# A retention layer with its FFN: the first 512 tokens as two units of 256, two tokens to a partition, and the FFN begun on the first unit

## The chip, the cores and the metric

The kernel runs on one core of one Trainium2 chip. The time is the device time of an execution in microseconds (us). Before the change the median of three runs is 356.64 us (356.58 to 357.01). Beside the times there is one profiled execution, from which every duration below is read.

## What is computed

Eight batches of 576 tokens with eight heads of 64 channels go through retention (attention without a softmax, the scores weighted by a power of the distance), and the result through a bilinear FFN:

```python
scores = scale * np.matmul(q, k.transpose(0, 1, 3, 2))      # B, H, S, D = 8, 8, 576, 64
gamma = 1.0 - 2.0 ** (-5.0 - np.arange(H))
rel = pos[:, None] - pos[None, :]
Dmat = np.where(rel >= 0, gamma[:, None, None] ** rel[None], 0.0)
attn = np.matmul(scores * Dmat[None], v)
x = attn.transpose(0, 2, 1, 3).reshape(B * S, H * D)        # 4608 x 512
out = ((x @ w_a) * (x @ w_b)) @ w_out                       # 512 -> 1536 -> 512
```

Inputs and output are float32; the products run in bfloat16.

## The kernel before

**Retention by chunks.** The 4608 tokens are 36 chunks of 128 tokens, a chunk two half steps of 64; nine half steps are a batch. The decay is factored: row j of v is multiplied by gamma to the power -j (table `vs`), row i of the result by gamma to the power i (table `qs`), so that only a 0/1 mask (`keep`) stands between. For a chunk, `load_qk` brings q and k with a cast to bf16 (GpSimd's queue), `load_v` brings v in float32 (SyncE's queue), `vscale` makes `vb` from `vf` and `vs`, `transposes` turns q and k over (by TensorE and two copies in the first chunks, by a DMA transpose on SyncE's queue from chunk 6), and `kv` forms k'v for each half step. The sums of these over a batch are the state: each sum (`s`, on VectorE, in a pool of three buffers) is cast to bf16 (`sbf`). `stage1` takes the products of q with the state and the scores `sc`, which VectorE masks into `sT`; `stage2` adds the products of `sT` with `vb` and the rest of the state products, and VectorE multiplies with `qs` into `xT`, the FFN's input, transposed. `kv` leaves its sums in a list `later`; `pop` takes one off at set places in the FFN, `flush` takes all.

**FFN by blocks.** Nine blocks of 512 tokens. `ffn_ab` runs twelve groups: four products with `wa_sb` into `pa`, cast by ScalarE into `ha`; four with `wb_sb` into `pb`; VectorE multiplies the two into `hT`. `ffn_out` takes four rows of 128 tokens with twelve products each into `po`, copied to `osb` by ScalarE and VectorE in turn and stored by SyncE. All of `pa`, `pb`, `po` and the transposes `tp` share four PSUM buffers (tag `ab`).

**What sets the order.** Each engine does its instructions in the order in which the program writes them. The front (chunks 0 to 3) is written out: four chunks one after the other, with `idle_products` (products of zeros) before and after, `hold` (a tiny DMA that makes SyncE's queue wait for a load), and the weights in four pieces of `load_w`. Then a table `todo` of (cost, function, unit) is worked off while the FFN runs: `run` adds up the cost of each product (1.0 for 512 columns) and calls the functions whose cost is reached at the next edge. Chunks 4 and 5 are units of their own, from 6 on a unit is two chunks:

```python
todo = [(52, begin_single, (4,)), (58, first, (4,)), (68, second, (4,)),
        (56, make_qs, (EARLY, QCOLS)),
        (80, begin_single, (5,)), (86, first, (5,)), (94, second, (5,)),
        (130, first, (6,)), (150, second, (6,))]
```

`begin_single` is vscale, transposes and kv of a chunk; `first` is stage1 and, through `ahead`, the transposes of the next unit, vscale of the one after on GpSimd, and loads of the fourth after; `second` is stage2 and kv of the next unit. A block has 144 such cost units: 96 of `ffn_ab`, 48 of `ffn_out`.

## Time and profile before

| What | us |
|---|---|
| median of three runs | 356.64 |
| profiled execution, in all | 358.02 |
| its span, first to last instruction | 356.3 |
| first FFN product | 28.28 |
| block 2 begins | 114.89 |
| last `ffn_out` begins | 342.20 |

The span is what the views divide up. TensorE (PE) is busy for 329.1 us of it, VectorE (DVE) 167.6, ScalarE (ACT) 93.5, GpSimd (POOL) 133.4. A busy TensorE is not one at its peak: the same product can take twice as long, which shows in the distance between starts and not in the share. In rows of the timeline the first two numbers are start and length in us, the brackets give the idle time before and what ended it; in rows of groups the numbers behind the bar are busy us, mean ns of one, and idle time before with its releasers.

### The profile page before, as it was taken

Reading aid. Unit: us, or ns where it says so; the run is one execution under the profiler, and the core shown is the slowest. Engines: PE = TensorE matmul, PEld = TensorE weight load, DVE = VectorE, ACT = ScalarE, POOL = GpSimd, SP = SyncE. Lnnn points to the kernel's source line nnn. Section 1 sums busy time; section 2 is a strip of 40 time slices with the busy share of each in tenths; the row PEclk is TensorE's granted clock in tenths of the full one; section 3 lists DMA queues with packets and bytes.
Section 4 is the critical chain, followed back from the end, with each engine's and each line's share of the span. In section 5 each row is a group of like instructions: output and inputs, shape, how many; then the busy total and the mean of one; then the engine's idle time right before and its main releaser. Section 6 shows DMA issues by size and latency. Waiting matters only on the chain.

```text
span 356.3 us, 8899 instructions
## 1 busy us (share of the span) xinstructions
PE 329.1 (92%) x3739; PEld 168.3 (47%) x3739; DVE 167.6 (47%) x321; ACT 93.5 (26%) x179; POOL 133.4 (37%) x196
## 2 busy tenths in 40 slices
PE   5559877599999999999999999999999999999995
PEld 2433434584774444444444445444444444444442
DVE  4652445343573456445553554464436534533321
ACT  3621363231220331132113211321232022212321
POOL 8765528932544604920554066307400310100000
PEclk9999999889999999999999999999999999999999
DMA  9999999999999990996199929966930140011002
GB/s 112 181 195 184 180 186 154 161 162 148 134 155 218 159 138 8 177 165 127 43 170 157 111 36 196 156 89 86 177 65 2 61 119 2 2 67 53 2 29 89
DMA packets 155624, 41.48 MB, mean 116 GB/s; under 512 B 145216, under 2 KB 151104, under 8 KB 155584
## 3 DMA queue, kind: packets, MB, share of 16 engines
q0 software_dynamic: 80944, 14.16, 51.2%
q1 hardware_dynamic: 74496, 26.62, 38.5%
q8 instruction: 29, 0.48, 0.5%
q10 hardware_dynamic: 144, 0.13, 0.1%
q14 instruction: 11, 0.09, 0.1%
HBM read 37.75 MB, written 9.44 MB: 132 GB/s over the span
## 4 chain that ended last, share of the span: by engine, by line
PE 84%; DMA 4%; DVE 4%; POOL 3%; issue 3%; ACT 1%; POOLq 0%; SPq 0%; DVEq 0%
PE pa L365 26%; PE pb L373 26%; PE po L390 25%; DMA vf<-in_v_dram 3%; POOL qk L102 2%; PE o L332 2%; PE o L290 2%; PE kv L257 2%; DVE s L270 1%; DMA qk<-in_q_dram 1%; PE sc L310 1%; DVE hT L378 1%; ACT qs L193 1%; DVE vb L219 1%; POOL vb L219 1%
## 5 line engine op out<-in xcount | busy, mean ns | idle before, releaser
L378 DVE TENSOR_TENSOR hT<-ha,pb 128x512 bf16<-128x512 bf16 (+2 forms) x126 | 76.9, 611 | 107.5 <-PE pb L373 100.5
L365 PE MATMUL pa<-xT,wa_sb 128*128 128x512 bf16 (+2 forms) x504 | 117.6, 358 | 4.7 <-DVE hT L378 3.9
L373 PE MATMUL pb<-xT,wb_sb 128*128 128x512 bf16 (+2 forms) x504 | 116.5, 355 | 0.0
L370 ACT CAST ha<-pa 128x512 bf16<-128x512 f32 (+2 forms) x126 | 66.0, 525 | 159.7 <-PE pa L365 159.6
L390 PE MATMUL po<-wo_sb,hT 128*128 128x512 bf16 x432 | 97.3, 379 | 0.0
L277 POOL CAST sbf<-s 128x256 bf16<-128x256 f32 x53 | 21.0, 403 | 154.7 <-DVE s L270 103.8
L373 PEld LDWEIGHTS <-wb_sb 128*128 128x128 bf16 x504 | 49.4, 101 | 47.4 <-issue 1.9
L365 PEld LDWEIGHTS <-wa_sb 128*128 128x128 bf16 x504 | 47.6, 101 | 48.8 <-issue 6.5
L390 PEld LDWEIGHTS <-hT 128*128 128x128 bf16 x432 | 41.1, 98 | 47.6
L102 POOL DMA_DIRECT2D qk<-in_q_dram x40 | 35.0, 877 | 8.5 <-issue 4.0
L102 POOL DMA_DIRECT2D qk<-in_k_dram x40 | 34.2, 859 | 8.0 <-DMA qk<-in_q_dram 4.9
L406 ACT COPY osb<-po 128x512 f32<-128x512 f32 x18 | 10.6, 586 | 80.1 <-PE po L390 80.1
L408 DVE COPY osb<-po 128x512 f32<-128x512 f32 x17 | 11.8, 692 | 41.5 <-PE po L390 41.5
L219 POOL TENSOR_TENSOR vb<-vf,vs 128x512 bf16<-128x512 f32 x30 | 30.6, 1039 | 0.0
L349 DVE TENSOR_TENSOR xT<-o,qs 128x512 bf16<-128x512 f32 (+1 forms) x42 | 23.8, 608 | 8.7 <-PE o L290 4.5
L318 DVE TENSOR_TENSOR sT<-sc,keep 128x512 bf16<-128x512 f32 (+1 forms) x42 | 23.8, 609 | 7.7 <-PE sc L310 7.6
L270 DVE TENSOR_TENSOR s<-kv,s 128x256 f32<-128x256 f32 x56 | 23.6, 421 | 7.0 <-POOL sbf L277 4.0
L290 PE MATMUL o<-qkT,sbf 64*64 64x64 bf16 x512 | 16.2, 201 | 7.3 <-DVE xT L349 5.0
L290 PEld LDWEIGHTS <-sbf 64*64 64x64 bf16 x512 | 10.9, 111 | 14.2 <-ACT sbf L275 5.6
L257 PE MATMUL kv<-vb,qk 64*64 64x64 bf16 x512 | 9.9, 203 | 6.5 <-DVE vb L219 5.4
L332 PEld LDWEIGHTS <-vb 64*64 64x64 bf16 x576 | 7.8, 113 | 10.4 <-issue 10.4
L332 PE MATMUL o<-sT,vb 64*64 64x64 bf16 x576 | 10.1, 200 | 2.5 <-DVE sT L318 2.4
(44 smaller groups left out, 92.5 us busy)
## 6 DMA issues: line engine op xcount, KB each, us to landing
out_dram<-osb SPq DMA_DIRECT2D x35, 256.0 KB, 2.8
vf<-in_v_dram SPq DMA_DIRECT2D x32, 256.0 KB, 6.1
qk<-in_q_dram POOLq DMA_DIRECT2D x32, 128.0 KB, 6.2
qk<-in_k_dram POOLq DMA_DIRECT2D x32, 128.0 KB, 7.0
wo_sb<-in_moe_w_out_dram POOLq DMA_DIRECT2D x3, 512.0 KB, 16.1
vf<-in_v_dram SPq DMA_DIRECT2D x8, 128.0 KB, 5.4
wa_sb<-in_moe_w_a_dram POOLq DMA_DIRECT2D x4, 192.0 KB, 8.0
wb_sb<-in_moe_w_b_dram POOLq DMA_DIRECT2D x4, 192.0 KB, 8.2
```

The costliest lines, as they stand in the source:

```text
L102: nc.gpsimd.dma_start(t[r0:r0 + n, w, :].rearrange("p (h d) -> p h d", h=H), src[b, :, s0:s0 + n, :].rearrange("h s d -> s h d"))
L219: eng.tensor_tensor(vb.rearrange("p (h d) -> p h d", h=H), vf.rearrange("p (h d) -> p h d", h=H), vs[:, i % PER, :].unsqueeze(2).to_broadc ...
L270: nc.vector.tensor_tensor(new, ps[s][:, ci], last_sum[0], op=ALU.add)
L290: nc.tensor.matmul(o[s][half(c), ci, j, :], st[half(r), p, :], qkt_of[i][half(r), 0, p, half(s)], start=start, stop=True, skip_group_check ...
L318: nc.vector.tensor_tensor(sT[:, r].rearrange("p n c t -> p (n c) t"), sc[r].rearrange("p n c t -> p (n c) t"), keep.unsqueeze(1).to_broadc ...
L332: nc.tensor.matmul(o[s][half(c), ci, j, :], vb[half(s), 64 * h:64 * h + 64], sT[half(s), h % 2, ci, h // 2, :], start=False, stop=True, sk ...
L349: nc.vector.tensor_tensor(view(xT, t0), o[s].rearrange("p n j t -> p j n t"), view(qs, c0), op=ALU.mult)
L365: nc.tensor.matmul(pa[:, 0:n], wa_sb[:, c, fs], xT[:, c, tok0:tok0 + n], start=(c == 0), stop=(c == NC - 1))
L370: nc.scalar.copy(ha[:, 0:n], pa[:, 0:n])
L373: nc.tensor.matmul(pb[:, 0:n], wb_sb[:, c, fs], xT[:, c, tok0:tok0 + n], start=(c == 0), stop=(c == NC - 1))
L378: nc.vector.tensor_tensor(hT[:, F, off:off + n], ha[:, 0:n], pb[:, 0:n], op=ALU.mult)
L390: nc.tensor.matmul(po, hT[:, F, u * 128:(u + 1) * 128], wo_sb[:, F, :], start=(F == 0), stop=(F == NF - 1))
```

## The change

The first 512 tokens (all of batch 0, bar its last 64) are no longer four chunks but two units u of 256 tokens, with two neighbouring tokens on a partition, so that a row of a load is 128 floats instead of 64. Everything for them has functions of its own (`fresh_...`). Their states are summed in PSUM (`kv_sum`) and cast by ScalarE from there. v of all chunks is loaded on GpSimd's queue instead of SyncE's, and `vf`, `vb` get more buffers. The FFN's groups 0 to 2 (`NF1 = 3`) run on unit 0, then on unit 1, in 256 columns; from group 3 on block 0 runs in 512. Chunks 4 and 5 move from `ffn_ab` of block 0 into its `ffn_out`, block 1's first half runs as twelve groups of 256 in place of twelve of 128 and six of 256, and each `first` and `second` gets a new place. `transposed` and `scale_v` are the DMA transposes and GpSimd's vscale of a unit; in `todo` a unit's number from 6 on is that of a pair, number 6 being chunks 6 and 7, number 7 chunks 8 and 9. kv now runs two units ahead, its casts one step after their sums. Identity, masks and ramps are made by VectorE's compares and by GpSimd ramps in float32.

```diff
-    vf_pool = pool("vf", 5)
-    vb_pool = pool("vb", 6)
+    vf_pool = pool("vf", 6)
+    vb_pool = pool("vb", 8)
...
     def load_v(i):
...
-            nc.sync.dma_start(
+            nc.gpsimd.dma_start(
...
+    load_fresh_v(0, 0, 4, nc.sync)
+    load_fresh_qk(0)
+    ramp(idx[:, 0:512], [[1, 512]], 0, 0)
+    ramp(posf[:, 0:4], [[1, 2], [256, 2]], 0, 2)
+    ramp(posf[:, 4:4 + MID + 1], [[128, MID + 1]], 0, 1)
+    load_fresh_v(0, 4, 8, nc.gpsimd)
+    ramp(posf[:, 4 + MID + 1:NPOS], [[128, PER - MID - 1]], 64, 1)
+    load_fresh_qk(1)
+    load_fresh_v(1, 0, 8, nc.gpsimd)
+    load_w(0, 128)
+    load_w(128, 384)
+    load_w(384, 768)
...
+    nc.vector.tensor_scalar(identity, idx[:, 0:128], rowf[:, 2:3], None,
+                            op0=ALU.is_equal)
...
-    idle_products(7)
-    for i in range(4):
-        vscale(i, nc.vector)
-        transposes(i, False)
-        kv((i,), nc.scalar)
-        flush()
...
+    NF1 = 3
+    idle_products(36)
+    fresh_vscale(0, 0, 4)
+    fresh_transposes(0, idle_products)
+    idle_products(8)
+    make_qs(256, 512)
+    fresh_scores(0)
+    fresh_kv(0, 0)
+    idle_products(4)
+    fresh_state1(0)
+    fresh_kv(0, 1)
+    ramp(idx[:, 512:S], [[1, S - 512]], 512, 0)
+    load_w(768, 1152)
+    load_w(1152, DFF)
+    idle_products(8)
+    fresh_transposes(1, None)
+    idle_products(4)
+    fresh_vscale(1, 0, 8)
+    settled(0)
+    fresh_stage2(0)
+    idle_products(4)
+    fresh_scores(1)
+    fresh_kv(1, 0)
+    run_all(ffn_ab(0, 0, 256, 0, 1))
+    fresh_state1(1)
+    fresh_kv(1, 1)
+    state_of[8] = fresh_state[4]
+    run_all(ffn_ab(0, 0, 256, 1, NF1))
+    settled(1)
+    fresh_stage2(1)
+    run_all(ffn_ab(0, 256, 256, 0, NF1))
...
+    load_wo(0, NF)
...
     def first(g):
         flush()
         stage1(units[g])
-        ahead(g)
+        if g >= 6:
+            if g + 2 < len(units):
+                transposed(g + 2)
+                scale_v(g + 2)
+            if g + 3 < len(units):
+                load(*units[g + 3])
...
     def second(g):
...
-        if 6 <= g + 1 < len(units):
-            kv(units[g + 1], nc.gpsimd)
+        if 8 < g + 2 < len(units):
+            kv(units[g + 2], nc.gpsimd)
...
+    load(*range(4, 10))
+    todo = [(60, make_qs, (512, S)), (64, make_qs, (S, 2 * S)),
+            (68, make_qs, (2 * S, QCOLS)),
+            (104, begin_single, (4,)), (110, first, (4,)), (118, second, (4,)),
+            (124, begin_single, (5,)), (130, first, (5,)),
+            (138, second, (5,)),
+            (139, scale_v, (6,)), (139, transposed, (6,)),
+            (140, load, (10, 11)), (145, scale_v, (7,)),
+            (148, kv, (units[6], nc.scalar)), (150, transposed, (7,)),
+            (166, first, (6,)), (180, second, (6,)),
+            (188, kv, (units[7], nc.scalar)),
+            (208, kv, (units[8], nc.scalar))]
...
-            todo += [(p - 86, first, (g,)), (p - 66, second, (g,))]
+            todo += [(p - 64, first, (g,)), (p - 50, second, (g,))]
...
-            todo += [(p - 40, first, (g,)), (p - 20, second, (g,))]
+            todo += [(p - 34, first, (g,)), (p - 18, second, (g,))]
...
-    at = [0.0]
-    run(ffn_ab(0, 0, 512, 0, NF))
-    run(ffn_ab(1, 512, 128, 0, 6))
-    run(ffn_ab(1, 640, 128, 0, 6))
-    run(ffn_ab(1, 512, 256, 6, NF))
+    at = [8.0 * NF1]
+    run(ffn_ab(0, 0, 512, NF1, NF))
     run(ffn_out(0))
+    run(ffn_ab(1, 512, 256, 0, NF))
     run(ffn_ab(1, 768, 256, 0, NF))
```

Three places in the order show what moves. The first is VectorE's queue up to the FFN's first `hT`. Before, the last of four chunks stands there (`vb`, its transposed k, two sums, the `xT` of the chunk ahead, two masks of its own, its `xT`):

```order
L219 TENSOR_TENSOR vb<-vf,vs 128x512
L241 COPY qkT<-tp 128x512
L270 TENSOR_TENSOR s_493<-kv_475,s_400 128x256
L270 TENSOR_TENSOR s_497<-kv_476,s_493 128x256
L349 TENSOR_TENSOR xT<-o_430,qs 128x4x64
L349 TENSOR_TENSOR xT<-o_431,qs 128x4x64
L318 TENSOR_TENSOR sT<-sc_537,keep 128x256
L318 TENSOR_TENSOR sT<-sc_538,keep 128x256
L349 TENSOR_TENSOR xT<-o_527,qs 128x4x64
L349 TENSOR_TENSOR xT<-o_528,qs 128x4x64
```

In the changed kernel the same queue holds unit 0's masks (`fsT`), unit 1's v (`fvb`), unit 0's `xT`, unit 1's masks, then the first three `hT`:

```order
L493 COPY fT<-ftp 128x1024
L546 TENSOR_TENSOR fsT<-fsc_280,keep_165 128x512
L546 TENSOR_TENSOR fsT<-fsc_281,keep_165 128x512
L546 TENSOR_TENSOR fsT<-fsc_301,keep_165 128x512
L546 TENSOR_TENSOR fsT<-fsc_302,keep_165 128x512
L462 TENSOR_TENSOR fvb<-vf_106,vs_all 128x512 x2
L568 TENSOR_TENSOR xT<-fo_344,qs 128x4x128
L568 TENSOR_TENSOR xT<-fo_345,qs 128x4x128
L546 TENSOR_TENSOR fsT<-fsc_482,keep_165 128x512
L546 TENSOR_TENSOR fsT<-fsc_483,keep_165 128x512
```

The sums have left VectorE, its instructions are twice as wide, and the masks of unit 1 stand between the first `xT` and the first `hT`.

The second place is GpSimd's queue around the first products on v. Before, from the scaled v of chunks 6 to 9 on (`qk` are loads of chunks 12 and 13, `vb` the scaled v, `sbf` casts of the state):

```order
L219 TENSOR_TENSOR vb<-vf,vs 128x512 x4
L102 DMA qk<-in_q_dram 128x8x64
L102 DMA qk<-in_k_dram 128x8x64
L102 DMA qk<-in_q_dram 64x8x64 x2
L102 DMA qk<-in_k_dram 64x8x64 x2
L277 CAST sbf<-s_1064 128x256
```

In the changed kernel, from the scaled v of chunks 8 to 11 on, with the loads of the same chunks 12 and 13:

```order
L246 TENSOR_TENSOR vb<-vf,vs_all 128x512 x4
L110 DMA vf<-in_v_dram 128x8x64
L102 DMA qk<-in_q_dram 128x8x64
L102 DMA qk<-in_k_dram 128x8x64
L110 DMA vf<-in_v_dram 64x8x64 x2
L102 DMA qk<-in_q_dram 64x8x64 x2
L102 DMA qk<-in_k_dram 64x8x64 x2
L246 TENSOR_TENSOR vb<-vf,vs_all 128x512 x2
```

Each chunk has a third load on this queue, v's, ahead of its q and k; `vb` is made for two chunks more ahead of these loads, and the first casts have gone behind them (ScalarE makes the earliest ones).

The third place is SyncE's queue at the first transposes by DMA. Before, they stand behind loads of v and ahead of any store:

```order
L110 DMA vf<-in_v_dram 128x8x64 x7
L231 DMA_TRANSPOSE qkT<-qk 128x8x128 x2
L110 DMA vf<-in_v_dram 128x8x64
L110 DMA vf<-in_v_dram 64x8x64 x2
L231 DMA_TRANSPOSE qkT<-qk 128x8x128 x2
```

In the changed kernel:

```order
L131 DMA vf_106<-in_v_dram 128x4x128
L448 DMA out_dram<-osb 128x512 x3
L258 DMA_TRANSPOSE qkT<-qk 128x8x128 x2
L448 DMA out_dram<-osb 128x512
L258 DMA_TRANSPOSE qkT<-qk 128x8x128 x6
```

The loads of v are gone from it, and the transposes of chunks 6 and 7 come behind three of block 0's four stores.

More of the change, by code (lines that the diff above doesn't have):

```diff
@@ new lines, in fresh_kv @@
+    def fresh_kv(u, s):
+        for p in range(HP):
+            for e in (0, 1):
+                for r in (0, 1):
+                    h = 2 * p + r
+                    nc.tensor.matmul(
+                        kv_sum[half(r), 64 * p:64 * p + 64],
+                        fresh[u][1][half(s), h, e, :],
+                        fv[u][e][half(s), 64 * h:64 * h + 64],
+                        start=(u == 0 and s == 0 and p == 0 and e == 0),
+                        stop=True, skip_group_check=True)
+        sb = sbf_pool.tile([128, HP, 64], BF16, tag="sbf", name="sbf")
+        nc.scalar.copy(sb, kv_sum[:, 0:256].rearrange(
+            "p (c t) -> p c t", c=HP))
+        fresh_state[2 * u + s + 1] = sb
@@ L455, in begin_single, with scale_v, transposed @@
         flush()
[L457 to L468 removed]
+    def scale_v(g):
+        for i in units[g]:
+            vscale(i, nc.gpsimd)
+    def transposed(g):
+        for i in units[g]:
+            transposes(i, True)
     def first(g):
```

295 lines of the change are left out of this document (192 added, 103 removed).

## The prediction

> **What bounds the kernel now.** I read the page first, the share of the span by engine and the chain that ended last, then the busy time by stage, then TensorE's timeline in blocks 0 and 1.
>
> ```profile
> span 356.3 us, 8899 instructions
> ...
> PE   5559877599999999999999999999999999999995
> ...
> DMA  9999999999999990996199929966930140011002
> ...
> PE 84%; DMA 4%; DVE 4%; POOL 3%; issue 3%; ACT 1%; POOLq 0%; SPq 0%; DVEq 0%
> ```
>
> TensorE is busy in nine tenths of every slice after the first eight or so; the chain is TensorE for 84%. The busy time by stage (stretch, length, then PE, PEld, DVE, ACT, POOL, clock, DMA, GB/s) says where the rest lies:
>
> ```profile
> 0.00:28.28 28.28, 15.33 (x300) 9.33 (x300) 15.63 (x48) 10.59 (x25) 21.01 (x38) 1.00 1.42 164
> 42.98:61.60 18.62, 12.92 (x209) 6.68 (x207) 10.41 (x22) 8.78 (x14) 10.22 (x12) 1.00 1.83 172
> 61.60:79.69 18.09, 14.24 (x204) 12.93 (x194) 7.63 (x23) 5.30 (x18) 13.15 (x18) 0.81 1.76 163
> 114.89:149.54 34.65, 34.38 (x393) 16.37 (x392) 17.65 (x30) 8.21 (x14) 16.54 (x24) 1.00 0.92 121
> 149.54:184.26 34.72, 34.45 (x401) 16.43 (x400) 17.32 (x29) 8.21 (x14) 12.58 (x18) 1.00 0.96 125
> ```
>
> Blocks 2 and 3 take 34.7 us each with TensorE full: nothing is to be had there. Before 28.28 no FFN runs, and blocks 0 and 1 take 114.89 - 28.28 = 86.6 us where two steady blocks would take 69.4. The timeline (start, length, instruction, idle before it and its releaser) shows the losses:
>
> ```profile
> 28.28 1.86 PE L365 MATMUL pa<-xT,wa_sb 128*128 128x512 bf16 x4 [0.85 <-DVE xT L349]
> 34.34 1.03 PE L365 MATMUL pa<-xT,wa_sb 128*128 128x512 bf16 x4
> 35.21 1.03 PE L373 MATMUL pb<-xT,wb_sb 128*128 128x512 bf16 x4
> 44.59 0.31 PE L257 MATMUL kv<-vb,qk 64*64 64x64 bf16 x8 [1.00 <-DVE vb L219]
> 51.32 0.62 PE L332 MATMUL o<-sT,vb 64*64 64x64 bf16 x16 [2.44 <-DVE sT L318]
> 61.35 0.32 PE L257 MATMUL kv<-vb,qk 64*64 64x64 bf16 x16 [0.68 <-POOL vb L219]
> 63.48 0.39 PE L365 MATMUL pa<-xT,wa_sb 128*128 128x128 bf16 x4
> 63.70 0.39 PE L373 MATMUL pb<-xT,wb_sb 128*128 128x128 bf16 x4
> 68.90 0.59 PE L365 MATMUL pa<-xT,wa_sb 128*128 128x128 bf16 x4 [3.85 <-DVE hT L378]
> 70.13 0.63 PE L373 MATMUL pb<-xT,wb_sb 128*128 128x128 bf16 x4
> 70.56 0.63 PE L365 MATMUL pa<-xT,wa_sb 128*128 128x128 bf16 x4
> 77.06 0.61 PE L365 MATMUL pa<-xT,wa_sb 128*128 128x256 bf16 x4
> 77.50 0.60 PE L373 MATMUL pb<-xT,wb_sb 128*128 128x256 bf16 x4
> ```
>
> Four products of 512 take 35.21 - 34.34 = 0.87 us, of 256 columns 0.44. From 28.28 to 34.34 stand sixteen products of 512, worth 3.46 us: the array ran slow, a loss of 2.6. After the wait of 3.85 the step is 0.43 (70.13 to 70.56) where it was 0.22 (63.48 to 63.70); that lasts 68.90 to about 74 and costs 2.5. Waits: 2.44, 3.85, and four for vb at chunks 4 to 7 (first and last shown), 3.15 together. Losses in blocks 0 and 1: 2.6 + 2.5 + 2.44 + 3.85 + 3.15 = 14.5; full-speed work 86.6 - 14.5 = 72.1 us.
>
> **The change, part by part.** Durations and transfers that I use:
>
> ```profile
> L318 DVE TENSOR_TENSOR sT<-sc,keep 128x512 bf16<-128x512 f32 x30 | 19.3, 685 | 5.8 <-PE sc L310 5.8
> L349 DVE TENSOR_TENSOR xT<-o,qs 128x512 bf16<-128x512 f32 x30 | 19.3, 685 | 7.2 <-PE kv L257 4.1 <-PE o L290 2.9
> L378 DVE TENSOR_TENSOR hT<-ha,pb 128x256 bf16<-128x256 bf16 x18 | 7.6, 420 | 6.0 <-PE pb L373 5.6
> L219 DVE TENSOR_TENSOR vb<-vf,vs 128x512 bf16<-128x512 f32 x6 | 4.1, 688 | 1.2 <-DMA vf<-in_v_dram 1.2
> L176 DVE TENSOR_SCALAR idxp_f<-idxp_f 64x1 f32<-64x1 f32 x1 | 0.1, 150 | 0.0
> L241 DVE COPY qkT<-tp 128x512 bf16<-128x512 bf16 x6 | 2.5, 421 | 2.2 <-ACT qkT L240 2.2
> L240 ACT COPY qkT<-tp 128x512 bf16<-128x512 bf16 x6 | 3.5, 582 | 8.4 <-PE tp L238 8.4
> L193 ACT ACTIVATE qs<-idx_f,biasq,lgp 128x768 f32<-128x768 f32 x4 | 3.8, 1016 | 0.2 <-DVE idx_f L191 0.2
> L193 ACT ACTIVATE qs<-idx_f,biasq,lgp 128x512 f32<-128x512 f32 x4 | 2.9, 801 | 0.0
> ...
> L219 POOL TENSOR_TENSOR vb<-vf,vs 128x512 bf16<-128x512 f32 x30 | 30.6, 1039 | 0.0
> L277 POOL CAST sbf<-s 128x256 bf16<-128x256 f32 x53 | 21.0, 403 | 154.7 <-DVE s L270 103.8 <-DVE s L268 41.2 <-ACT osb L406 7.8
> L102 POOL DMA_DIRECT2D qk<-in_q_dram x40 | 35.0, 877 | 8.5 <-issue 4.0 <-PE pa L365 1.4 <-DMA wa_sb<-in_moe_w_a_dram 1.0
> ```
>
> ```profile
> q0 software_dynamic: 5822, 0.73, 230.6%
> ...
> q0 software_dynamic: 1355, 0.98, 127.8%
> ...
> 1.44 1.08 POOL L102 DMA_DIRECT2D qk<-in_q_dram  x1 [0.32 <-issue]
> ...
> 5.17 0.61 PE L238 MATMUL tp<-identity,qk 128*128 128x128 bf16 x4 [0.75 <-DMA qk<-in_q_dram]
> ```
>
> Supply first. The first row is 55 to 60 us, chunk loads alone: 1024 packets are one q or k load, 5822 in 5 us are 0.88 us a load. The second is 20 to 25 us, mostly weights: 0.98 MB written as bf16 are 1.96 MB read, 392 GB/s. The packets of the fresh loads are 512 bytes instead of 256; I take the weights' rate (chunk rate: 0.4 us more a load): 0.52 MB in 1.35 us. Today q lands 3.7 us after its issue began (1.44 to 5.17). Now POOL issues it some 0.5 us sooner and it is twice as large: q at about 5.4, k 6.7, the second half of v 7.4, then 8.8, 10.1 and 11.5 for unit 1. Weights (6.3 MB) end at 27.5, wo (3.1) at 35.5, chunks 4 to 9 (18 loads of 0.88) at 51.4. Each is needed later than that (below), so supply hides.
>
> The front is a chain on VectorE, in the order of its rows. Eleven small instructions that make identity and masks by compares stand first; the trace has none of them, so between 0.15 (the 64x1 row) and 0.42 (256 columns) each, from about 4.0, when POOL has issued two loads and made the ramps: to 5.7 or 8.6. I take 5.7, since most are a column or 128 wide; the other end delays the chain by 1.2. Then v's second half at 7.4, scaled in 2 x 0.42 (8.2); copy of kT, 2 x 0.42 (9.1); first scores (9.6); four masks of 0.685 (12.3); unit 1's v, 2 x 0.69 (13.7). Beside it TensorE does state, transposes of unit 1 and the second stage of unit 0, about 14.9. Then xT, 2 x 0.685 (16.3), four masks of unit 1 (19.0), hT 0.42. The three first FFN groups of 256 (0.87 each) fit between, with their pb waiting for score buffers and hT: 21.1. Second stage, 48 products of 128 columns (sixteen of 64 show 0.32 at 61.35, so 0.8 to 1.9): 1.2; xT 1.37 (23.7), three groups on unit 1 2.6: 26.3. With 1.0 allowed for some fifteen handovers between engines: **27.3 us when group 3 starts at 512 columns**. Today group 3 starts at 34.34 + 1.73 = 36.07: 8.8 us sooner.
>
> What remains of blocks 0 and 1: 72.1 - 3 x 1.73 = 66.9; six groups of 256 columns (0.87) in place of twelve of 128 (0.44) change nothing. One more pair's kv lies in block 1 and one fewer at the end: nothing in sum.
>
> New or kept waits:
> - make_qs. At the edge at cost 64 ACT gets four of 64 and four of 576 columns, at 72 four of 128. From the rows, 0.95 for 768 and 0.73 for 512 give 0.30 + 0.00084 per column: 1.4 + 3.1 = 4.5 us, then 1.6. Groups need ha every 1.73 and own two pairs of PSUM buffers, 3.46 us: TensorE waits 1.4, then 0.45. **1.9** (today's 2.44 came from the same 3.8).
> - Chunks 4 and 5 now run inside ffn_out(0), with eight products (1.73 us) between steps. vb has no hT ahead of it, so the four waits of 3.15 go. The chain from tp, ACT copy 0.58, DVE copy 0.42, sum 0.42 (like the copy), cast 0.40 (as POOL's), is about 2.0 with its handovers: **0.3 twice**. A steady block's 34.65 less 144 products of 0.217 leaves 1.7 for each of its two pairs; I take a single chunk at 1.3.
> - DMA transposes of chunks 6 and 7 stand on SP behind three output stores:
>
> ```profile
> L231 SPq DMA_TRANSPOSE qkT<-qk x30: 1231/1444/3893, 61.9 to 290.1; - x30
> ...
> DMA to landing us min/median/max: 3.1/6.3/10.2
> ```
>
>   ffn_out(0) begins at 27.3 + 15.6 + 1.9 = 44.8; the third store goes at about 55.8, the second transpose 1.4 to 3.9 later, landing 6.3 after (63.5 to 66); first(6), after 10.4 of ffn_out, two singles of 1.6, six groups and kv(6), wants it at about 64. Between 0 and 6 (the slowest landing): **1.0**.
> - DVE in ab(1) with adds between hT (0.42 + 0.42 per 0.87): 0 to 2, **0.5**.
>
> v on POOL costs 2 x 0.88 us more issue per pair; a pair's POOL work becomes 2 x 1.04 + 6 x 0.88 + four casts of 0.4 = 9.0 us in half a block, 17 us, so it hides. Loads end at 51, vb(6) and vb(7) two POOL products later, and kv(6) wants them at about 44.8 + 10.4 + 3.2 + 0.9 = 59; chunk 4 lands at 38 and is wanted at 46.5. Later placings (first and second 16 units apart, 3.5 us, against masks of 1.4) leave blocks 2 to 8 as they are.
>
> Sum: block 2 starts at 27.3 + 66.9 + 1.9 + 0.6 + 1.0 + 0.5 = 98.2 instead of 114.89: **-16.7 us**. The profiled execution took 358.02 us (span 356.3 and 1.7 around it), the median of the runs is 356.64, nearer to the span. I take the difference off the median: 356.64 - 16.7 = **339.9 us** (a profiled execution would then show 341.3).
>
> **A rule against the trace.** The half-rate stretches above (0.43 against 0.22 a step, after a wait of 3.85) are the row. The Trainium skill, "TensorE: Matmul & The Clock Gate", section on the HAM clock gate, says that the array runs at half rate until it was busy through one free-running window of about 3.4 us. By that rule the 36 small idle products and the transposes after them, nearly unbroken to about 8.5, warm it for good, and the sum stays at 339.9; going by today's front, which never warms, it is 343 to 344, the first rival.
>
> **Rivals.**
> 1. The array stays at half rate through the front, as it does today until about 34, idle products and all. For: VectorE's chain leaves TensorE gaps of 1 to 1.5 us. Against: small idle products fill most. Price: unit 1's groups 2.6 more, the first 512 groups up to 1.7: 343 to 344. Chance 0.22.
> 2. A wait like the 3.85 in block 1 comes back (loads, POOL's vb, or the transposes at their slowest landing) and cools the array: 3.85 + 2.5: about 346. For: the DMA row stays near 9 until past 100 us. Against: 6 us of slack at vb(6), 8 at chunk 4. Chance 0.15.
> 3. Slower than before: POOL's queue. At the second unit of a block vb and six load issues (2 x 1.04 + 6 x 0.88 = 7.4 us) stand ahead of the casts of kv; VectorE's fourth sum needs the first cast's buffer (s32 has three), and hT stands behind it. Today's 0.88 per issue leaves 1 us there and two pairs of PSUM buffers another 1.2; from 1.25 us an issue TensorE waits, and at 1.65 seven blocks lose 2.4 each, all of the gain. The slowest issue in the rows is 1.08. Chance 0.04. The Trainium skill, "SBUF — State Buffer", warns of it (box on "DVE blocks DMA"): POOL cannot write descriptors while VectorE holds the shared port, and an issue of 620 ns took 3100. By that figure, an estimate, blocks would lose some 11 us each; the 0.88 mean over 40 issues beside a busy VectorE shows no such hold.
>
> **How the numbers follow.** Forecast 0.59: 339.9, own range 336.5 (waits at their lower ends) to 342.5 (a slower front by 2.5). With rivals 1 and 2 the range is 336 to 346. A difference under 0.2% (0.7 us) could not be told from none. Faster 0.95, same 0.01, slower 0.04.
>
> **What would show it.** First FFN product near 17, group 3 near 27, at steps of 0.87; make_qs waits near 36 to 41; ffn_out(0) near 45; block 2 near 98, then 34.7 a block. Wrong if steps of 0.43 for four of 128 (1.73 for 512) go on after 20, if q lands after 6, if a wait over 3 us stands before block 2, or if casts on POOL precede waits for hT in blocks 2 to 7.

## The result and the profile after

| | median us (range) | ratio to before, 95% interval |
|---|---|---|
| before | 356.82 (356.58 to 358.23) | |
| changed kernel | 344.29 (342.33 to 344.59) | 0.9625 [0.9572, 0.9678] |
| changed kernel, again | 343.91 (340.52 to 344.05) | 0.9615 [0.9559, 0.9671] |
| forecast | 339.9 (336.0 to 346.0) | |

The profiled execution of the first comparison took 1866.62 us, its products at about a sixth of their rate from end to end (1.32 us for one of 512 columns, not 0.22); why is open. The profile here is therefore that of the repetition (execution 344.05 us, span 342.3). Medians, ranges and ratios, here and below, leave out executions over 1.5% above the fastest of their kernel, whose times are given beside them.

The page of the changed kernel has these slices and this chain that ended last (lines left out are marked by dots):

```profile
span 342.3 us, 8911 instructions
...
PE   6788899899999999999999999999999999999995
...
PEclk9869999989999999999999999999999999999999
DMA  9999999999999909990999099909990500020002
...
PE 89%; DMA 4%; ACT 2%; DVE 2%; issue 1%; POOL 1%; POOLq 0%; DVEq 0%
```

From the third slice on TensorE is busy for eight tenths or more of each slice, where before it had slices of five and seven tenths up to the eighth. But the granted clock dips three times (second, third and ninth slice). The busy time by stage (columns as above: stretch, length, PE, PEld, DVE, ACT, POOL, granted clock, DMA, GB/s) puts bounds to that:

```profile
0.00:18.68 18.68, 12.92 (x293) 11.12 (x294) 10.91 (x45) 9.50 (x16) 15.67 (x30) 0.89 1.24 174
4.36:7.77 3.41, 1.64 (x34) 1.20 (x34) 2.52 (x11) 3.12 (x7) 3.41 (x6) 1.00 1.64 220
7.77:11.19 3.42, 3.06 (x72) 2.62 (x68) 2.01 (x5) 1.94 (x4) 3.42 (x6) 0.50 1.66 218
14.60:18.01 3.41, 1.78 (x81) 1.40 (x72) 1.48 (x4) 0.99 (x2) 3.41 (x7) 1.00 1.28 167
18.01:24.84 6.83, 6.16 (x49) 4.12 (x48) 3.26 (x7) 1.71 (x5) 4.36 (x8) 0.50 1.25 186
69.21:72.63 3.42, 3.42 (x54) 2.50 (x39) 1.71 (x3) 0.60 (x2) 2.20 (x3) 0.50 1.70 139
102.75:136.92 34.17, 34.17 (x394) 16.26 (x393) 17.21 (x29) 8.19 (x14) 17.35 (x23) 1.00 0.95 123
136.92:171.13 34.21, 34.21 (x393) 16.28 (x392) 17.21 (x29) 8.19 (x14) 18.89 (x26) 1.00 0.94 126
```

And TensorE's timeline (start, length, instruction, idle before) answers to the rows of before:

```profile
16.21 0.36 PE L558 MATMUL fo<-fsT,fvb 64*64 64x128 bf16 x10 [1.44 <-issue]
18.68 1.01 PE L404 MATMUL pa<-xT,wa_sb 128*128 128x256 bf16 x4 [0.86 <-DVE fsT L546]
19.49 1.06 PE L412 MATMUL pb<-xT,wb_sb 128*128 128x256 bf16 x4
27.03 0.60 PE L404 MATMUL pa<-xT,wa_sb 128*128 128x256 bf16 x4 [1.38 <-DVE xT L568]
27.46 0.60 PE L412 MATMUL pb<-xT,wb_sb 128*128 128x256 bf16 x4
29.64 1.03 PE L404 MATMUL pa<-xT,wa_sb 128*128 128x512 bf16 x4
43.08 1.02 PE L404 MATMUL pa<-xT,wa_sb 128*128 128x512 bf16 x4 [1.19 <-ACT ha L409]
46.82 1.89 PE L429 MATMUL po<-wo_sb,hT 128*128 128x512 bf16 x8
55.42 0.32 PE L284 MATMUL kv<-vb,qk 64*64 64x64 bf16 x16 [0.32 <-DVE vb L246]
69.00 0.25 PE L329 MATMUL o<-qkT,sbf 64*64 64x64 bf16 x8 [2.03 <-DMA qkT<-qk]
69.56 1.04 PE L404 MATMUL pa<-xT,wa_sb 128*128 128x256 bf16 x4
70.39 1.06 PE L412 MATMUL pb<-xT,wb_sb 128*128 128x256 bf16 x4
86.03 0.44 PE L349 MATMUL sc<-qkT 64*64 64x64 bf16 x30 [0.65 <-DVE s L297]
```

The first FFN product stands at 18.68 instead of 28.28, group 3 at 29.64 (forecast 27.3), `ffn_out(0)` at 46.82 (44.8), block 2 at 102.75 (98.2; before 114.89). From 18.7 to 24.8 four products of 256 take 0.81 to 0.85 us (18.68 to 19.49 and on) instead of 0.43 (27.03 to 27.46): this is half rate, and it comes once more behind the wait at 69.00. A first stretch at half rate, 7.77 to 11.19, lies ahead of the FFN, behind the waits for q and k (1.19 and 0.58 us). From block 2 on TensorE waits for nothing, and blocks 2 to 4 take 34.2 us instead of 34.7.

So 12.1 of the 14.0 us of span that were gained come before block 2, and 1.9 after it.

### The profile page after: what moved, and what is told of

It is laid out like the page before. It is cut to its first block, busy times and chain, and to the rows that moved or that the text cites. A ratio compares the mean times of both kernels' runs of the same rounds, so it can differ in the third digit from the quotient of the medians.

```text
span 1864.8 us, 8870 instructions
## 1 busy us (share of the span) xinstructions
PE 1820.3 (98%) x3733; PEld 561.5 (30%) x3774; DVE 168.4 (9%) x320; ACT 98.4 (5%) x188; POOL 157.5 (8%) x216
## 4 chain that ended last, share of the span: by engine, by line
PE 98%; issue 2%; DVE 0%; ACT 0%; DVEq 0%
PE pb L412 31%; PE pa L404 30%; PE po L429 29%; PE o L329 1%; PE sc L349 1%; PE idle_ps L585 1%; PE kv L284 1%; PE o L371 1%; PE ftp L482 1%; PE kv_sum L502 0%; PE fo L558 0%; PE fsc L537 0%; PE tp L265 0%; PE fo L515 0%; DVE xT L568 0%
## 5 line engine op out<-in xcount | busy, mean ns | idle before, releaser
L412 PE MATMUL pb<-xT,wb_sb 128*128 128x512 bf16 (+1 forms) x491 | 618.0, 1538 | 1.9 <-issue 1.9
L404 PE MATMUL pa<-xT,wa_sb 128*128 128x512 bf16 (+1 forms) x477 | 600.2, 1537 | 14.5 <-issue 13.1
L429 PE MATMUL po<-wo_sb,hT 128*128 128x512 bf16 x407 | 548.9, 1699 | 23.1 <-issue 23.1
L412 PEld LDWEIGHTS <-wb_sb 128*128 128x128 bf16 x492 | 154.4, 314 | 414.2 <-issue 413.9
L404 PEld LDWEIGHTS <-wa_sb 128*128 128x128 bf16 x492 | 154.8, 317 | 394.7 <-issue 394.0
L429 PEld LDWEIGHTS <-hT 128*128 128x128 bf16 x432 | 124.4, 293 | 379.4 <-issue 379.4
L417 DVE TENSOR_TENSOR hT<-ha,pb 128x512 bf16<-128x512 bf16 (+1 forms) x123 | 76.6, 622 | 1060.0 <-PE pb L412 1060.0
L409 ACT CAST ha<-pa 128x512 bf16<-128x512 f32 (+1 forms) x123 | 65.6, 533 | 1170.3 <-PE pa L404 1161.8
L110 POOL DMA_DIRECT2D vf<-in_v_dram x36 | 31.9, 888 | 129.0 <-DVE vb L246 127.8
L329 PEld LDWEIGHTS <-sbf 64*64 64x64 bf16 x456 | 24.9, 286 | 37.1 <-issue 26.2
L246 POOL TENSOR_TENSOR vb<-vf,vs_all 128x512 bf16<-128x512 f32 x30 | 30.7, 1044 | 51.9 <-ACT vs_all L196 36.6
```

The lines of the kernel that those rows point to most:

```text
L110: nc.gpsimd.dma_start(t[r0:r0 + n, :].rearrange("p (h d) -> p h d", h=H), v[b, :, s0:s0 + n, :].rearrange("h s d -> s h d"))
L246: eng.tensor_tensor(vb.rearrange("p (h d) -> p h d", h=H), vf.rearrange("p (h d) -> p h d", h=H), vs[:, i % PER, :].unsqueeze(2).to_broadc ...
L329: nc.tensor.matmul(o[s][half(c), ci, j, :], st[half(r), p, :], qkt_of[i][half(r), 0, p, half(s)], start=start, stop=True, skip_group_check ...
L404: nc.tensor.matmul(pa[:, 0:n], wa_sb[:, c, fs], xT[:, c, tok0:tok0 + n], start=(c == 0), stop=(c == NC - 1))
L409: nc.scalar.copy(ha[:, 0:n], pa[:, 0:n])
L412: nc.tensor.matmul(pb[:, 0:n], wb_sb[:, c, fs], xT[:, c, tok0:tok0 + n], start=(c == 0), stop=(c == NC - 1))
```

## The experiments

Where each stood at the two marks of the forecast, and the time between them, read from TensorE's timeline (us; one profiled execution each; the times come with the experiments):

| kernel | group 3 | block 2 | between |
|---|---|---|---|
| before | 36.07 | 114.89 | 78.82 |
| changed | 29.64 | 102.75 | 73.11 |
| new front, old order behind it | 26.99 | 117.49 | 90.50 |
| no FFN groups on 256 columns | 30.96 | 106.49 | 75.53 |
| no idle products | 26.02 | 101.92 | 75.90 |
| more idle products | 28.52 | 100.32 | 71.80 |
| qs spread | 27.89 | 101.87 | 73.98 |
| transposes early | 26.17 | 101.16 | 74.99 |
| transposes on TensorE | 27.02 | 99.50 | 72.48 |
| v on SP | 32.22 | 101.62 | 69.40 |
| places of before | 28.83 | 106.48 | 77.65 |
| three edits | 27.33 | 95.83 | 68.50 |
| three edits, no idle products | 29.43 | 97.52 | 68.09 |

Group 3 falls between 26.2 and 29.6 in the seven profiles that share the changed kernel's front, so a difference of 3 us at one mark between two single profiles shows nothing by itself.

**The changed kernel again.**

> The changed kernel as it is, for a profile in which TensorE's products take their usual time (in the one at hand a product of 512 columns takes 1.3 us throughout). If the forecast's terms hold but for size, the time is 342 to 345, group 3 of block 0 starts between 27 and 31, block 2 between 98 and 104, and later blocks take 34.7. If the array stays at half rate through the front (rival 1), quads of 128x512 products step by 1.7 us instead of 0.87 past 27. If a wait like the old 3.85 came back (rival 2), one idle stretch of over 3 us stands between 45 and 100.

343.91 (340.52 to 344.05). The time, group 3 and block 2 fell into the theory's ranges; blocks 2 to 4 came shorter than expected (34.2 for 34.7). By their marks both rivals fail: from group 3 on four products of 512 step by 0.87, and the longest wait between 45 and 100 is 2.03. Of the FFN's products in the front only unit 0's groups ran at half rate, unit 1's did not.

**The front alone.** Everything behind the new front is placed as before:

```diff
-    todo = [... (104, begin_single, (4,)), (110, first, (4,)), ...
+    todo = [(52, begin_single, (4,)), (58, first, (4,)), (68, second, (4,)), ...
+            (130, first, (6,)), (150, second, (6,))]
...
+    run(ffn_ab(1, 512, 128, 0, 6))
+    run(ffn_ab(1, 640, 128, 0, 6))
+    run(ffn_ab(1, 512, 256, 6, NF))
     run(ffn_out(0))
-    run(ffn_ab(1, 512, 256, 0, NF))
```

> The new first 512 tokens with the placing of before for everything behind them (chunks 4 and 5 inside block 0, block 1 begun in units of 128 before ffn_out(0), pairs one ahead). Theory: the front's 6.4 us (group 3 of block 0 at 29.64 instead of 36.07) are mostly lost again, because chunk 4's q and k land only at 41.5 and its transposes are now wanted at about 36: a wait of 4 to 6 us appears at chunk 4 in block 0, and the waits of before at block 1 stay. Span 350 to 355, median 351 to 355. Rival: the two parts add, the front alone gives its 6.4: median 349.5 to 350.5.

(Dots mark what is left out here; `ahead` and `second` are as before too, and v stays on GpSimd's queue.)

Median 357.33 (354.71 to 359.78; three more executions took 360.68, 363.18 and 1160.04), ratio 1.000 [0.996, 1.004]: nothing is left of the front's gain. The profile is that of the execution of 360.68, so it shows some 3 us more loss than the median has. Four of TensorE's waits in it:

```profile
41.33 0.58 PE L265 MATMUL tp<-identity,qk 128*128 128x128 bf16 x4 [7.26 <-DMA qk<-in_q_dram]
...
52.15 0.64 PE L371 MATMUL o<-sT,vb 64*64 64x64 bf16 x16 [3.69 <-DVE sT L357]
57.75 0.32 PE L284 MATMUL kv<-vb,qk 64*64 64x64 bf16 x16 [1.01 <-DVE vb L246]
69.23 0.38 PE L412 MATMUL pb<-xT,wb_sb 128*128 128x128 bf16 x4 [2.65 <-DVE hT L417]
```

Group 3 begins 9.1 us sooner than before, and chunk 4, now wanted at 34, is waited for 7.26 us; the qs wait (3.69) and that for hT (2.65) of before are there again. The theory's mechanism holds; its size was too small: the wait was 7.26 for 4 to 6, the median 2.3 above its upper end (355). In this profile the clock was at half from 38.97 to 45.80 and three times more, which I had not counted. So the front gains nothing without the new order behind it, and the two parts do not add. What the new order gains without the new front was not tried.

**No FFN groups on the first unit.**

```diff
-    run_all(ffn_ab(0, 0, 256, 0, 1))
...
-    run_all(ffn_ab(0, 0, 256, 1, NF1))
...
-    run_all(ffn_ab(0, 256, 256, 0, NF1))
...
-    at = [8.0 * NF1]
-    run(ffn_ab(0, 0, 512, NF1, NF))
+    at = [0.0]
+    run(ffn_ab(0, 0, 512, 0, NF))
```

> The two units of 256 stay, but the three FFN groups on 256 columns go: block 0 runs all twelve groups at 512 after both units. Theory: the front's end is set by VectorE's chain and by half-rate products, and the groups on the first unit delay the second unit's second stage (it started at 24.90, behind products at half rate from 18.68); without them it starts at 20.5 to 21.5 and xT(1) is done by 23: group 3 starts between 27.6 (full rate) and 30.5 (half rate), against 29.64, and the median is within 342 to 345, no clear change. Rival: starting the FFN on the first unit is worth the 2.6 us of its three groups: group 3 at 32, median 346 to 347.

346.45 (343.3 to 347.9), 0.9691 [0.963, 0.9753]. The interval overlaps that of the changed kernel. In this profile:

```profile
23.94 0.58 PE L404 MATMUL pa<-xT,wa_sb 128*128 128x512 bf16 x1 [1.39 <-DVE xT L568]
...
25.60 1.91 PE L412 MATMUL pb<-xT,wb_sb 128*128 128x512 bf16 x4
27.31 1.23 PE L404 MATMUL pa<-xT,wa_sb 128*128 128x512 bf16 x4
...
30.96 1.03 PE L404 MATMUL pa<-xT,wa_sb 128*128 128x512 bf16 x4
```

The first product on the second unit did come sooner (23.94 for 27.03), as the theory has it, but half rate (25.60 to 27.31 for four products) and three whole groups then stand behind it: group 3 at 30.96, between the theory's 30.5 and the rival's 32, against 26.17 to 29.64 in the seven profiles that share the changed kernel's front. By the time the rival is nearer: the groups on the first unit are worth 1.3 to 4.8 us at this mark, and by the medians 2.5, which these intervals can't tell from none. Part of it is not theirs: this profile has three pauses more without a releaser than the changed kernel's, 1.44 in the front and 1.43 and 2.81 behind group 3.

**No idle products, and more of them.** In the first kernel all 68 go (the loop in `idle_products` runs 0 times), in the second there are 8 more ahead of `settled(0)`, 4 more behind `fresh_stage2(0)` and 14 ahead of the first FFN group.

> All idle products leave the front. Theory: the array then has no busy window before the FFN's groups, all products of the front run at half rate, and VectorE's chain hides part of it; group 3 starts at 30 to 32, median 345 to 347. Rival 1: the idle products pay nothing because the array cools anyway: group 3 at 29 to 30, median 343 to 344.5. Rival 2: half-rate lasts on into block 0's 512-column groups as in the kernel before (until 33.6): group 3 above 32 and the median above 347.

> 26 more idle products of 128 columns in the front: 8 ahead of the second stage of unit 0, 4 behind it, 14 ahead of the first FFN group. Two questions. The pause without a releaser (1.2 to 2.0 us after 22 of the 32 fo products in the five-term runs so far): if it hangs on a number of TensorE instructions (their code being fetched), it moves with the 8 new instructions, to after about 14 of the 32; if it is a wait of that place, it stays after 22. The clock: theory: TensorE's pauses before 18 us cool it; with the pauses of 0.86 and some of the others filled, the half-rate stretch of 18.01 to 24.84 is absent and group 3 starts at 26 to 27.5 in place of 29.64, median 341 to 343 (it is 343.9 for the changed kernel, and its gain can be eaten by loads that then come too late, as the run with early transposes showed). Rival: the pause alone cools it, group 3 stays at 29 to 30.

Without: 344.33 (342.93 to 345.7), 0.9643 [0.9586, 0.970]. With more: 342.35 (341.52 to 342.38, and one of 346.67), 0.9628 [0.9548, 0.9708]. No difference in time to the changed kernel can be told for either. But without them group 3 began at 26.02, the earliest of all, with the clock full from 15.22 on: the theory of the first falls. Rival 1's time came (343 to 344.5), its reason did not, since the clock stayed full once it was. In the second the half-rate stretch at the FFN's first groups is gone, as its theory says, though another stands at 12.25 to 15.66. Group 3 stands at 28.52, not 26 to 27.5; I put that down to 26 products more, that stretch and the pause, which moved, but did not part them. The pause in the two kernels:

```profile
17.71 0.22 PE L502 MATMUL kv_sum<-fvb,fqk 64*64 64x64 bf16 x2 [1.21 <-issue]
```

```profile
21.75 0.19 PE L502 MATMUL kv_sum<-fvb,fqk 64*64 64x64 bf16 x1 [1.29 <-issue]
```

In the changed kernel it stands after 22 of 32 `fo` products, ahead of the 224th recorded product. Without idle products there are 64 fewer ahead of that place, and the pause stands 64 products further on in the program (10 and 8 `fo`, 32 scores, 14 of `kv_sum`), so ahead of the 224th again. With 8 more it does not show where I expected it (after 14 `fo`), but 127 recorded products behind that. In the kernel without early groups it shows twice, 128 products apart. In ten of the twelve profiles with this front it stands ahead of the 224th. It hangs on the count of TensorE's instructions, in steps of 128 products.

**qs spread.**

```diff
-    todo = [(60, make_qs, (512, S)), (64, make_qs, (S, 2 * S)),
-            (68, make_qs, (2 * S, QCOLS)),
+    todo = [(40 + 8 * j, qs_part, (j, S, 2 * S)) for j in range(NC)]
+    todo += [(72 + 4 * j, qs_part, (j, 512, S)) for j in range(NC)]
+    todo += [(84 + 4 * j, qs_part, (j, 2 * S, QCOLS)) for j in range(NC)]
```

> The twelve qs instructions of chunks 4 and later are issued one or two to an FFN group (cost 40 to 96) instead of twelve within two groups. Theory: the wait of 1.19 us at 43.08 (pa <- ACT ha) and the 0.3 after it are ScalarE's 4.46 and 1.65 us standing ahead of ha; spread, they fit into the 1.2 us that ScalarE has free in each group, ffn_out(0) starts 1.3 to 1.5 earlier than in the changed kernel's run (46.82), and the median is 342.4 to 342.7. Rival: what is gained is given back at the wait for the DMA transposes at 69.00, which come no sooner: that wait is 3.3 to 3.5 instead of 2.03 and the median stays at 343.5 to 344.3.

(`qs_part` makes one of the instructions of `make_qs`.) 343.15 (341.41 to 343.24, and one of 347.65), 0.9595 [0.9546, 0.9644], which overlaps the changed kernel's interval. The wait for ha is gone: from group 3 to `ffn_out(0)` it took 15.54 us, in the changed kernel 17.18, so 1.64 less, a little more than the 1.3 to 1.5 expected. It is given back, but not where the rival looked: the wait for the DMA transposes is 1.31, shorter than the changed kernel's 2.03. On TensorE, VectorE and GpSimd of this kernel:

```profile
53.97 0.32 PE L290 MATMUL kv<-vb,qk 64*64 64x64 bf16 x16 [2.25 <-DVE vb L252]
```

```profile
51.30 2.62 DVE L252 TENSOR_TENSOR vb<-vf,vs_all 128x512 bf16<-128x512 f32 x1
```

```profile
51.19 2.16 POOL L252 TENSOR_TENSOR vb<-vf,vs_all 128x512 bf16<-128x512 f32 x2
```

Chunk 5's vb, 0.69 us by itself, took 2.62 while GpSimd made two vb of its own; it ended 0.6 after they had. TensorE waited 2.25 for it and ran at half rate from 54.59 to 58.01. In the changed kernel VectorE's began at 54.68, after GpSimd's two.

**Transposes of chunks 6 and 7 earlier, and on TensorE.**

```diff
-            (139, scale_v, (6,)), (139, transposed, (6,)),
+            (100, transposed, (6,)), (139, scale_v, (6,)),
```

```diff
-            (139, scale_v, (6,)), (139, transposed, (6,)),
+            (139, scale_v, (6,)), (139, transposed_pe, (6,)),
```

(`transposed_pe` has the same chunks turned over by TensorE and two copies each.)

> The DMA transposes of chunks 6 and 7 are issued from cost 100 instead of 139, ahead of the output stores of block 0 on SP; their source q and k of chunk 7 landed at 50.9 and 51.7 us in the run before this. Theory: the order on SP made the wait of 2.03 us at 69.00 (o <- DMA qkT), and that wait made the half-rate stretch 69.21 to 72.63, worth another 1.5. Both go: first(6) starts without a DMA wait, block 2 starts at 99.2 instead of 102.75, the span is 338.5 to 339.5, the median 340 to 341 (from 343.9). Rival 1: the transposes are slow because they share the DMA engines with loads, wherever they are issued; a wait over 1 us stays and the median moves by less than 1. Rival 2: another wait takes the place (sums on VectorE); gain 1 to 2. Rival 3: the first transpose holds SP until k lands, the output stores come late and TensorE waits for an output buffer: no gain or slower.

> Chunks 6 and 7 are transposed by TensorE (sixteen products, two copies a chunk) instead of by DMA. Theory: they cost TensorE about 1.1 us and take two transposes out of the way of the loads of chunks 10 to 13; the wait of 2.03 us at first(6) and its half-rate stretch of 1.5 go, no wait for k takes their place as it did with the transposes issued early (2.01 and 0.98 us at kv): block 2 starts at 99.5 to 101 if the front is as slow as in the changed kernel's run (102.75), and the median is 341 to 342.5. Rival: the supply of chunks sets block 1's end whichever engine transposes: waits for vb or k of together 2 us or more appear in block 1, median within 1 of 343.9.

Early: 342.39 (340.24 to 343.29, and one of 345.71), 0.9572 [0.9499, 0.9645]; on TensorE: 341.53 (340.08 to 344.06), 0.9572 [0.9512, 0.9632]. Neither interval is clear of the changed kernel's. With the early ones the wait at `first(6)` is gone, but the timeline then has

```profile
85.11 0.31 PE L284 MATMUL kv<-vb,qk 64*64 64x64 bf16 x8 [0.98 <-DMA qk<-in_k_dram]
...
95.76 0.32 PE L284 MATMUL kv<-vb,qk 64*64 64x64 bf16 x16 [2.01 <-DMA qk<-in_k_dram]
```

and half rate from 97.08 to 100.49. Group 3 was 3.47 sooner than in the changed kernel, block 2 only 1.59. So rival 2 is nearest, with a DMA's wait in place of VectorE's: another wait takes the place. v of chunk 11, issued at 56.93 behind two transposes, landed after 13.3 us (6.4 in the changed kernel, issued at 56.01), and GpSimd's queue, which waits for it, issued the loads of chunks 12 and 13 at 71.4 instead of 63.5. With TensorE's transposes neither wait exists; block 2 begins at 99.5, within the theory's range. But the theory assumed a front as slow as the changed kernel's, and here group 3 began 2.6 sooner: between the marks this kernel takes only 0.6 us less, with a wait of 1.03 for vb and a pause of 1.44 that the changed kernel's profile does not have.

**v on SP.** `load_v` issues on `nc.sync` as it did before the change.

> The loads of v go back to SP, everything else as in the changed kernel. Theory: issuing v on POOL costs nothing on the path (POOL is busy 9 of 17 us a half block), so blocks 2 to 8 stay at 34.2 and the median within 1 of 343.9, unless SP's order (v behind output stores and transposes that wait) makes block 1 wait for v. Rival 1: POOL's issues delay the casts; without them blocks 2 to 8 get shorter by 0.2 or more each, median 342 or less. Rival 2: v behind waiting entries on SP comes late: a wait for vb over 1 us at kv, median above 345.

345.18 (342.57 to 346.22), 0.9665 [0.9645, 0.9686]. Blocks 2 to 6 stay at 34.17 to 34.18: GpSimd's issues delay no casts. The median is 1.3 above the changed kernel's, with intervals that overlap. What this order costs shows where neither theory nor rivals looked, at the very start; this kernel's timeline has

```profile
7.53 1.06 PE L482 MATMUL ftp<-identity,fqk 128*64 128x128 bf16 x16 [2.83 <-DMA fqk<-in_q_dram]
...
32.22 1.03 PE L404 MATMUL pa<-xT,wa_sb 128*128 128x512 bf16 x3
```

SP has nothing to wait for, issues v of chunk 4 at 1.24 us beside q, and q lands at 7.48 instead of 6.00. With the loads on GpSimd's one queue, in the order of need, q is not held up so. In this profile (342.57, the fastest of five) the late front is made up before block 2, which begins 1.13 sooner than in the changed kernel's: the transposes of chunks 6 and 7 landed 3.2 to 3.7 us after their issue, where they took 7.1 to 7.8, and nothing waited for them. So no run shows that the change gains by v's move to GpSimd's queue.

**Places of before for the units from 7 on** (`p - 86`, `p - 66`, `p - 40`, `p - 20`), sums still two pairs ahead.

> First and second stages of the units from 7 on stand where they stood before the change (22 and 16, 6 and 2 product groups earlier), the sums of keys and values stay two pairs ahead. Question: what shortened blocks 2, 3 and 4 from 34.65, 34.73 and 34.61 to 34.17 to 34.22. Theory: the sums being two pairs ahead takes away the waits for the cast states (o <- POOL sbf, 1.1 us in four); the blocks stay at 34.1 to 34.3. Rival: the placing did it; blocks 2 to 4 go back to 34.5 to 34.8.

One time, 349.76. Block 2 takes 34.33, blocks 3 to 6 take 34.61 to 34.64:

```profile
175.45:210.06 34.61, 33.90 (x388) 16.29 (x392) 17.13 (x29) 8.21 (x14) 17.35 (x23) 1.00 0.92 122
```

```profile
PE sc L349 <- DVE s L297: 1.0, 4, 0.2
```

The rival's number came, though not by the wait of before: the list of waits has no line for the cast states from block 2 on, so the sums two pairs ahead did take that away, as the theory says. In its place scores wait for VectorE's sums, whose PSUM buffers they share, once in each of blocks 3 to 6 (0.24 us), where first and second stand in the old places; the blocks are 0.43 longer, of which this list names half. The old places alone do not make a block long: before the change blocks 5 and 6 had no wait and took 34.17 and 34.13. It took both parts to have no wait from block 2 on; the new places with the sums one pair ahead were not tried.

**Three edits together:** transposes on TensorE, qs spread, and chunk 5's v scaled right behind chunk 4; and the same without idle products.

```diff
+            (106, vscale, (5, nc.vector)),
             (124, begin_single, (5,)), (130, first, (5,)),
```

> Three edits together: TensorE transposes chunks 6 and 7, the qs instructions are spread one or two to a group, and chunk 5's v is scaled right behind chunk 4 (cost 106), so that it no longer meets the two products of POOL beside which it took 1.39 to 2.62 us instead of 0.69. Theory: against the run with TensorE's transposes alone (median 341.5, span 339.1) the wait for ha (1.19) and that for vb at chunk 5 (1.03) go: span 336.5 to 337.5, median 338.5 to 340. Rival: the chunk loads set the end of block 1; what is gained in block 0 is waited for at kv or first there (vb, k or T), median 341 to 342.

> As the run with the three edits together, but without any idle product in the front. Theory: the idle products do not set the front's end (group 3 began at 26.02 without them, at 26.17 to 29.64 with them); the median is within 1.5 of that run's. Rival: without them the first FFN products fall at half rate more often: median 2 to 4 higher.

337.16 (335.9 to 338.21), 0.9425 [0.9404, 0.9447], and without idle products 337.35 (335.79 to 339.66), 0.9439 [0.9406, 0.9471]. Both beat the changed kernel, some 6.7 us, clear of its interval. Behind group 3 TensorE waits, by its list of waits, for

```profile
PE po L435 <- issue: 2.7, 17, 0.2
PE sc L355 <- DVE s L303: 0.6, 1, 0.6
```

(the first are gaps of 0.16 where the record lacks a product: it has 3748 for 3790 weight loads). Chunk 5's vb takes 0.68 on VectorE. From group 3 to block 2 it is 68.5 us, against 73.1 in the changed kernel and 70.9 in the forecast. It gave more than the 1.5 to 3 expected over the transposes alone; that profile also had a pause of 1.44 at `kv`, which this one has not, and I can't say how much of the rest is such luck. The third edit was not run by itself. The idle products again pay nothing.

## Why the prediction was right, and where it was off

The direction and the mechanism were right: the gain comes from FFN products that start 10 us sooner, from chunks 4 and 5 moved to where their loads have landed, and from waits of before in blocks 0 and 1 that do not come back (3.85 for hT and 3.15 for vb, of which 0.32 is left), or come back smaller (2.44 for qs). The size was not: 343.9 to 344.3 lies within 336 to 346, but outside the forecast's own 336.5 to 342.5, and only the two rivals had made the range so wide. Term by term, from one execution of the changed kernel:

| step | forecast | measured |
|---|---|---|
| group 3 at 512 columns | 27.3 | 29.64 |
| waits for qs | 1.9 | 1.6 |
| singles | 0.6 | 0.3 |
| DMA transposes of chunks 6, 7 | 1.0 | 2.03 + 1.5 at half rate |
| VectorE in `ab(1)` | 0.5 | 0.65 |
| block 2 begins | 98.2 | 102.75 |
| later blocks | 0 | -1.9 |

Block 2 came 4.55 late. That 1.9 came back behind it was luck, since no term had it. The rest of the 4 us is in how the forecast was put: the profiled execution of before was 1.4 above the median of its kernel, that of the changed kernel only 0.1, so 14.0 us between two profiles are 12.5 to 12.8 between medians.

One of the forecast's signs of being wrong did come, products at half rate after 20 (up to 24.84), and q landed at its limit, 6.00. No wait over 3 us stands before block 2, and no cast delays hT.

- **Front.** The chain on VectorE was near: the first FFN product at 18.68 for 17, with q at 6.00 for 5.4, masks of 2.48 for four (12.3 forecast, 13.0 measured). In the six other profiles with the same front code group 3 began at 26.17 to 28.83, on average of all seven at 27.7. In the one shown, half rate added 2.4 (six times four products at 0.83 for 0.43). That is rival 1 in part: its price for one unit (2.6), but on unit 0's groups, and the array had been at full rate from 11.19 to 18.01.
- **What failed there** is "warm it for good". The array was at full rate from 4.36, but the idle products and transposes were not "nearly unbroken to about 8.5": TensorE waited 1.19 for q and 0.58 for k, and the clock fell to half at 7.77. It fell again at 18.01, behind the pause of 1.44 and part of the wait of 0.86. The section on the clock gate in the Trainium skill's "TensorE: Matmul & The Clock Gate" lets the array cool after an idle window of about 3.4 us. The trace is stricter than the table of that page: here it cooled with no single pause longer than 1.44 (the last section has the bound).
- **Waits for qs.** The two ScalarE stretches are as computed (4.5 and 1.6); TensorE waited 1.19 and 0.13 and lost 1.6 in all, since the kernel with qs spread took 1.64 less for this stretch. ScalarE's rows:

```profile
38.09 4.46 ACT L223 ACTIVATE qs<-idx,biasq,lgp 128x64 f32<-128x64 f32 x8
42.46 0.56 ACT L409 CAST ha<-pa 128x512 bf16<-128x512 f32 x1
42.93 1.65 ACT L223 ACTIVATE qs<-idx,biasq,lgp 128x128 f32<-128x128 f32 x4
```

- **Transposes.** The right place, too small by 2.5. SP's queue in the changed kernel:

```profile
51.51 7.04 SPq L448 DMA_DIRECT2D out_dram<-osb  x3
58.68 5.86 SPq L258 DMA_TRANSPOSE qkT<-qk  x2
```

  The third store went at 58.22, not 55.8, the two transposes held SP for 5.86 us (2.4 and 3.4; I took 1.4 to 3.9) and the second landed at 68.95, not 63.5 to 66. And I priced the wait without the cooling that follows it, though the wait of 3.85 of before had shown that price.
- **Supply.** "Hides" held for weights and for chunks 4 to 9, with less room than I gave: chunk 4 landed at 41.5 (38) since wo, one transfer of 1.5 MB issued ahead of it on the same queue, landed at 38.84 (35.5), and chunk 9 at 57.82 (51.4). The early transposes, which made k late until 95.76, show that supply is no free resource up to there.
- **VectorE beside GpSimd.** The 0.69 for vb was right in this profile; in four others, where chunk 5's met GpSimd's two, it took 1.4 to 2.6. In two more it took 1.2 and 1.4 beside GpSimd's load issues alone, and why is open. The Trainium skill's "SBUF — State Buffer", section "SBUF: two separate sides", says that a VectorE operation with two inputs in SBUF and a GpSimd one that reads there exclude each other for a whole instruction; the rows of the kernel with qs spread agree (2.62 beside 2.16). I drew on that page for descriptors only, where its 620 and 3100 ns are those of a transfer alone and beside a VectorE copy. The trace again shows no such hold: 36 issues of v took 0.89 each on GpSimd.
- **Later blocks.** That "nothing is to be had there" was wrong. Sums two pairs ahead and new places take 0.4 to 0.5 off each of blocks 2 to 4, a gain that I passed over because the waits there looked too small to matter. From block 2 on TensorE's waits before were

```profile
PE o L290 <- POOL sbf L277: 1.1, 4, 0.3
```

  one each in blocks 2, 3, 4 and 7; blocks 5 and 6, without one, already took 34.17 and 34.13. Another 0.8 is block 7, which also has one pair's kv fewer, work that now lies in block 1.
- **Rival 3** did not happen: issues on GpSimd took 0.87 to 0.89 on average, and from block 2 on TensorE waited for no cast.

## What to carry to other kernels

A start-up that is made shorter pays only if what follows is placed by the landing of its loads: here the front alone gave nothing. After a change, list the waits that are left, and price each with the half rate that it may bring: removing three small ones (1.2 for ha, 2.0 for the transposes, and vb's, 0.3 to 2.3 by execution) gained 6.7 us, half of what the whole change had gained. And the same step should not be given to VectorE and GpSimd at the same time, even if each has time to spare: vb took up to 2.62 us in place of 0.69.

## What the runs showed of the hardware

- **The clock's window.** In each profile the granted clock changes at distances that are multiples of 3.41 us. I took the idle time of TensorE in each such window, up to the last block's `ffn_out`, in the twelve profiles of new kernels and that of before. Of the windows at full rate, 19 with 1.59 to 3.41 us of idle were followed by half rate, and those with up to 1.51 were not. Two do not fit: one with 1.29 (more idle products, 8.83 to 12.25) was followed by half rate, and one with 1.79 (before, 47.26 to 50.67) was not. So the bound for cooling is near half a window. To warm takes far more: half rate ended behind windows with 0.36 us of idle or less (20) and went on behind those with 0.52 or more (7). A single wait of 2.24 or 2.41 (more idle products, no idle products) that fell across two windows cooled nothing.

  Where the windows lie against the program differs between executions, and this goes with the times of one kernel: the changed one took 343.91 to 344.05 us at a mean granted clock of 0.980 to 0.985, and 340.52 at 0.994.
- **A pause at a 128th product**, 0.5 to 2.0 us in the front where it shows, 1.2 to 2.8 in block 1. The page of the changed kernel has 29 packets on a queue for instructions, and one of them moves in the 4 us around the pause (13 to 17 us):

```profile
q8 instruction: 1, 0.02, 1.5%
```

  Each of these packets has 16384 bytes. TensorE's 3774 products and as many weight loads are 29.5 times 256, so a packet holds 128 of each if an instruction has 64 bytes. The Trainium skill's "Perfetto Trace Analysis", section on the per-instruction lifecycle, gives that size.

  The packet of the changed kernel's pause runs from 13.75 to 14.69, the pause from 14.77 to 16.21. Of the 19 such pauses in the twelve profiles, 18 end 1.3 to 1.6 us after the end of a packet (the other 2.1). So TensorE waits there for its code; this rests on the count and on the times in the traces, and no run changed it on purpose.
